# An H3 convolution with a bilinear GLU, forward and backward: product splits taken back and the last stage's order exchanged

## The chip, the cores and the metric

The kernel runs on one core of one Trainium2 chip. The metric is the device time of one execution in microseconds (us), smaller is better; a kernel is timed several times and the median is given. The profile is one further execution, taken by the hardware profiler.

## The reference

With x of shape 2048 x 512 in bf16, the reference computes a layer, and then the gradients of all nine inputs for a given output gradient `grad_out`. Cut to what matters:

```python
def _A_ref(q, k, v, shift_k, ssm_k, ssm_D):        # S = 2048, D = 512
    k_shift = sum(k_pad[:, t:t+S, :] * shift_k[:, 3-t] for t in range(4))
    kv = k_shift * v
    y = irfft(rfft(kv, 2*S) * rfft(ssm_k, 2*S))[:S] + kv * ssm_D   # a causal convolution over time
    return q * y

def _B_ref(x, w_gate, w_up, w_down):               # F = 1376
    h = (x @ w_gate) * (x @ w_up)
    return h @ w_down

xn = layernorm(x)
out = x + _A_ref(xn, k, v, shift_k, ssm_k, ssm_D) + _B_ref(xn, w_gate, w_up, w_down)
out, vjp = jax.vjp(_f, ...); grads = vjp(grad_out)
```

There are ten outputs: the layer's output, and the gradients for x, k, v, shift_k, ssm_k, ssm_D and the three weights.

## The kernel before

**Layout.** The 2048 rows are held as 16 row groups of 128 (R = 16); two neighbouring groups are a pair, n = 0 to 7. One SBUF array, `big`, holds everything, and tiles are places in it. PSUM is one array, `PP`, of eight banks of 512 f32 columns.

**Stages.** They overlap.
- `mlp_rows(j, r)`: F is cut into six steps j (widths 256, 96, 256, 256, 256, 256). For a pair of row groups a step computes the gradient through `w_down` (`pd`) and the gate and up products (`pg`, 512 columns for both), copies them out of PSUM and multiplies them into a ring of tiles; `hd_store` sends most of them to the DRAM array HD.
- `dw_gen(j)`: the weight gradients of step j, sums of products over the 16 row groups.
- `a_gen`, `s_B`, `s_pw`, `s_Bi`: the convolution, forward and backward, as a discrete Fourier transform in three steps with smaller tiles of the array (64x128, 64x32, 32x64); the results go through the DRAM arrays AX and CX.
- The last stage, in pairs n: `c_load(n)` brings pair n's part of CX into the one buffer `C` (1.5 MB); `last_dft(n)` makes three results of it with 24 products of shape 128x32; `c_dkv`, `c_y`, `c_o5` take them out and go on with them on ScalarE and VectorE; `c_dsk(n)` sums over the rows with 8 products of shape 128x32; `dk_pair` makes the gradient of k on VectorE. `hd_load(n)` reads pair n's part of HD with a transposing DMA into one of two buffers (`hdP[n % 2]`), `turn_gen` turns what was kept in SBUF, and `y_o(n, rr)` (11 products of 512 columns) and `y_x(n, rr)` (22) make the output and the gradient of x for the two row groups rr of the pair. `y_load`, `dkv_load` and `k_load` bring the other operands of 256 KB.

**Order.** All instructions are first recorded as 2271 entries; a run of products into one PSUM place with the same due time is one entry. `emit(PLAN)` then unpacks the constant `PLAN`: the order in which the entries are issued, and the PSUM bank of each of the 398 PSUM places. Each engine works through its entries in that order; waits between engines follow from the data and from places used again. All DMAs are issued by SyncE (SP) in the plan's order:

```python
raw = zlib.decompress(base64.b85decode(plan))
order = struct.unpack(f"<{len(ops)}H", raw[:2 * len(ops)])
for s, b in zip(slots, raw[2 * len(ops):], strict=True):
    s.base = Q[b // 2] if s.n == 2 else halves[b]
```

**Splits and fillers.** In step 3, and in step 4 for r < 8, `mlp_rows` makes the `pg` product in two halves of 256 columns. Ahead of the first data, the fillers multiply a tile of ones by itself: four products of 512 columns and eight of 256, then smaller ones.

Of the kernel before, what the change touches and what calls it, by code (L numbers as in the profile page):

```python
# [38 lines left out]
def kernel(  # L39
# [38 lines left out]
    Q = [PP[:, 1024 * i:1024 * i + 1024] for i in range(4)]  # L78
# [127 lines left out]
    MM = nc.tensor.matmul  # L206
# [44 lines left out]
    ones1 = rc.tile("ones", [128, 128])  # L251
# [11 lines left out]
    XT = rT.tile("XT", [128, 16, 1024])  # L263
    xnT = XT[:, 0::2, :].rearrange("p g (h c t) -> p g h c t", h=2, c=4)
# [21 lines left out]
    kh = ra.tile("kh", [128, R + 3, D])  # L286
# [28 lines left out]
    def wgu(j):  # L315
        return Wl[j % 2][:, 4 * SW[j]:12 * SW[j]].rearrange("p (c f) -> p c f", c=4)
# [6 lines left out]

    at0 = rN("P")
    now[0] = -50.0
    for i in range(12):
        w = 4 if i < 4 else 2
        MM(at0[:, 0:128 * w], lhsT=ones1[:], rhs=ones1[:].unsqueeze(1).to_broadcast((128, w, 128)), start=True, stop=True)
    for i in range(8):
        now[0] = -40.0 + i  # L330
        MM(at0[:, 0:128], lhsT=ones1[:], rhs=ones1[:], start=True, stop=True)
# [85 lines left out]
    def mlp_rows(j, r):  # L417
        fw = SW[j]
        h = ring(j, r, 2)
        if j:  # L420
            g = gu[(8 * j + r // 2) % 2].rearrange("p r (t f) -> p r t f", t=3)
            d = g[:, :, 2:3, :fw]
        else:
            g = gu0[r // 2 % 3].rearrange("p r (t f) -> p r t f", t=2)
            d = h[:, :, 0:1, :fw]
        pd = v3(rN(), 2)
        for rr in range(2):
            for c in range(4):
                MM(pd[:, rr, :fw], lhsT=goT[:, r // 2, c, 128 * rr:128 * rr + 128], rhs=wdT(j)[:, c, :], start=(c == 0), stop=(c == 3))
        (VCOPY if j in (3, 4, 5) else ACOPY)(d[:, :, 0], pd[:, :, :fw])  # L430
        for rr in range(2):
            pg = rN()[:, 0:2 * fw]
            for p in (slice(0, fw), slice(fw, 2 * fw)) if j == 3 or j == 4 and r < 8 else (slice(0, 2 * fw),):
                for c in range(4):
                    MM(pg[:, p], lhsT=xnT[:, r // 2, rr, c, :], rhs=wgu(j)[:, c, p], start=(c == 0), stop=(c == 3))
            ACOPY(g[:, rr, 0:2, :fw], pg.rearrange("p (t f) -> p t f", t=2))
        TT(h[:, :, 1:3, :fw], d.to_broadcast((128, 2, 2, fw)), g[:, :, 0:2, :fw], op=ALU.mult)
        TT(h[:, :, 0, :fw], g[:, :, 0, :fw], g[:, :, 1, :fw], op=ALU.mult)
# [143 lines left out]
    f = {}  # L582
# [251 lines left out]
    F0, F1 = 240.0, 415.0  # L834
    O0, OJ = 230.0, 10.0
# [60 lines left out]
    A = Gen(a_all())  # L896
# [42 lines left out]
    for n in range(NCH):  # L939
        last = n + 1 == NCH  # L940
        t = F0 + n * DF
# [30 lines left out]
        else:  # L972
# [4 lines left out]
            if n + 2 < NCH:  # L977
                y_load(n + 2)
                hd_load(n + 2)
    emit(PLAN)  # L980

# [106 lines left out]
```

## Time and profile before

| what | us |
|---|---|
| median of 3 runs (lowest, highest) | 426.84 (425.93, 427.25) |
| the profiled execution's own time | 426.57 |
| its span, first to last instruction | 424.4 |
| TensorE products (PE), busy | 415.1 |
| VectorE (DVE), busy | 349.0 |
| ScalarE (ACT), busy | 261.5 |

The page has the busy time of each engine (part 1), the span in 40 slices of 10.6 us with the busy share in tenths (part 2), the chain of work that ended last (part 4), and the costliest groups of instructions (part 5). In a group's row, "x1228 | 288.9, 380" means 1228 instructions, 288.9 us busy together, 380 ns from start to end of one; products overlap, so the mean is longer than their spacing. In a row of waits, "2.1, 2, 1.7" is the sum in us, how many, and the longest. In a timeline row come the start, the duration, the engine and the instruction; "L173" is the helper line through which every instruction is issued, so the tiles tell what it is. "SPq" is SP's queue: the time in which it issues a DMA. "PEld" is the weight load of a product.

### The profile page before, as it was taken

To read this page: it belongs to the slowest core of one execution; us is meant where nothing else is said; L and a number is where in the kernel's file an instruction comes from. 1 tells how busy PE (TensorE), PEld (TensorE's weight loads), DVE (VectorE), ACT (ScalarE), POOL (GpSimd) and SP (SyncE) were. 2 spreads that over 40 slices of the span, in tenths; PEclk is the share of its full clock that TensorE was granted. 3 is DMA by queue.
4 is the path that set the end of the run, shared out by engine and by line. 5 is a ranking of instruction groups with operands and counts; after the bars stand their busy time and mean duration, and the time that the engine had idled before them with its cause. 6 is when DMAs were issued, how large, how long until landed. Compare 5 with 4: busy or idle time off the path is not lost.

```text
span 424.4 us, 8338 instructions
## 1 busy us (share of the span) xinstructions
PE 415.1 (98%) x3290; PEld 209.3 (49%) x3290; DVE 349.0 (82%) x653; ACT 261.5 (62%) x380; POOL 3.5 (1%) x9
## 2 busy tenths in 40 slices
PE   8999999999999999999999999999999899999995
PEld 5755555855675444544444344445444344444443
DVE  5999977998649989899999990325858799999996
ACT  4855988598644999888999953362525331323324
POOL 1000000000000000000000000000000000000000
PEclk9999999999999999999999999999999999999999
DMA  7989999999788869968878899999999999999964
GB/s 262 398 197 379 320 306 388 349 367 365 288 310 287 319 229 352 313 227 318 319 274 344 292 312 325 298 348 274 231 275 329 303 269 329 308 302 286 267 193 144
DMA packets 104366, 127.27 MB, mean 300 GB/s; under 512 B 63876, under 2 KB 74249, under 8 KB 103304
## 3 DMA queue, kind: packets, MB, share of 16 engines
q1 hardware_dynamic: 104328, 126.75, 93.5%
q8 instruction: 25, 0.41, 0.4%
q14 instruction: 13, 0.11, 0.1%
HBM read 57.10 MB, written 54.04 MB: 262 GB/s over the span
## 4 chain that ended last, share of the span: by engine, by line
PE 77%; DMA 10%; DVE 10%; issue 1%; SPq 1%; ACTq 0%; ACT 0%
PE PP L173 77%; DVE big L173 10%; DMA out_dram<-big 4%; DMA big<-CX 2%; DMA big<-in_k_dram 2%; SPq L173 1%; DMA big<-in_w_dram 1%; DMA big<-in_go_dram 1%; ACTq L1084 0%; ACT big L173 0%
## 5 line engine op out<-in xcount | busy, mean ns | idle before, releaser
L173 PE MATMUL PP<-big 128*128 128x512 bf16 (+8 forms) x3290 | 415.1, 345 | 4.3 <-DMA big<-CX 2.1
L173 PEld LDWEIGHTS <-big 128*128 128x128 bf16 (+4 forms) x3290 | 209.3, 97 | 209.7 <-issue 61.0
L173 DVE TENSOR_TENSOR big<-big 128x1024 bf16<-128x1024 bf16 (+2 forms) x465 | 267.7, 631 | 45.5 <-ACT big L173 36.6
L173 ACT CAST big<-PP 128x512 bf16<-128x512 f32 (+2 forms) x314 | 224.4, 780 | 82.1 <-PE PP L173 71.1
L173 ACT ACTIVATE big<-big 128x1 f32<-128x1 f32 (+3 forms) x46 | 23.6, 522 | 53.4 <-DVE big L173 50.5
L173 DVE CAST big<-PP 128x512 bf16<-128x512 f32 (+1 forms) x37 | 32.4, 875 | 9.8 <-PE PP L173 5.2
L173 ACT COPY big<-PP 128x1024 bf16<-128x1024 bf16 x15 | 14.9, 1010 | 18.3 <-PE PP L173 18.3
L173 DVE SCALAR_TENSOR_TENSOR big<-big 128x512 bf16<-128x512 f32 (+2 forms) x36 | 23.3, 654 | 0.2
L173 DVE SCALAR_TENSOR_TENSOR big<-big,PP 128x512 f32<-128x512 bf16 x14 | 9.6, 684 | 9.2 <-PE PP L173 9.2
L173 DVE BATCH_NORM_STATS2 big<-big 128x6 f32<-128x512 bf16 x16 | 10.6, 682 | 4.0 <-DMA big<-in_x_dram 3.9
L173 DVE TENSOR_TENSOR big<-big,PP 128x512 bf16<-128x512 bf16 x14 | 9.2, 683 | 1.5 <-PE PP L173 1.5
L173 POOL MEMSET big<- 128x1536 bf16 (+2 forms) x3 | 2.9, 950 | 252.4 <-PE PP L173 252.4
L173 DVE TENSOR_SCALAR big<-big 128x512 bf16<-128x512 bf16 (+1 forms) x13 | 4.6, 385 | 0.0
L173 ACT ACTIVATE big<-PP 128x512 f32<-128x512 f32 x2 | 1.2, 597 | 4.5 <-PE PP L173 4.5
L173 DVE BATCH_NORM_AGGREGATE big<-big 128x2 f32<-128x6 f32 x16 | 2.3, 169 | 0.1
L173 ACT ACT_TABLE_LOAD x1 | 1.3, 1283 | 0.7 <-PEq L1076 0.7
L173 DVE RECIPROCAL big<-big 128x2 f32<-128x2 f32 (+1 forms) x9 | 1.2, 151 | 0.6 <-ACT big L173 0.6
L173 DVE DVE_READ_ACCUMULATOR big<-big 128x1 f32 x16 | 1.3, 82 | 0.0
L173 DVE DVE_READ_ACCUMULATOR big<-big,PP 128x1 f32 x14 | 1.2, 82 | 0.0
L173 DVE MEMSET big<- 128x128 bf16 (+1 forms) x2 | 0.2, 112 | 0.8 <-PEq L1076 0.8
L173 DVE COPY big<-PP 128x1024 bf16<-128x1024 bf16 x1 | 0.7, 692 | 0.2 <-PE PP L173 0.2
L173 ACT ACTIVATION_READ_ACCUMULATOR big<-PP 128x1 f32 x2 | 0.4, 194 | 0.0
(6 smaller groups left out, 0.9 us busy)
## 6 DMA issues: line engine op xcount, KB each, us to landing
HD<-big SPq DMA_DIRECT2D x32, 384.0 KB, 5.4
AX<-big SPq DMA_DIRECT2D x16, 768.0 KB, 5.6
big<-AX SPq DMA_DIRECT2D x16, 768.0 KB, 6.0
CX<-big SPq DMA_DIRECT2D x16, 768.0 KB, 5.4
out_dram<-big SPq DMA_DIRECT2D x43, 256.0 KB, 3.8
big<-CX SPq DMA_DIRECT2D x7, 1536.0 KB, 8.0
big<-in_vK_dram SPq DMA_DIRECT2D x8, 512.0 KB, 5.1
big<-in_w_dram SPq DMA_DIRECT2D x4, 768.0 KB, 7.5
```

Source lines behind the costliest of these rows:

```text
L173: o.fns.append(lambda: f(*[fix(x) for x in a], **{kk: fix(x) for kk, x in k.items()}))
```

## The change

Three edits:
- The splits of the `pg` products are taken back: one product of 512 columns for each of the four parts c, in all steps.
- The first fillers are eight products of 512 columns.
- `PLAN` is another one. Unpacked, the first 1575 of its 2271 entries stand in the same order with the same PSUM banks; behind them, every engine's and SP's order is another one, and 55 of the later PSUM places have another bank. It was chosen by its mean over drawn courses of the execution. No work is added or left out apart from the splits.

```diff
-PLAN = "c-l=@V-RM$vTb+9wr$(CZQHhO+qP}nHjZbGjlseD...
+PLAN = "c-l=@V-zMyuZ~k=+qP}nwr$(CZQHhOn~Rw>XV#ee...
...
-    for i in range(12):
-        w = 4 if i < 4 else 2
-        MM(at0[:, 0:128 * w], lhsT=ones1[:], rhs=ones1[:].unsqueeze(1).to_broadcast((128, w, 128)), start=True, stop=True)
+    for i in range(8):
+        MM(at0[:, 0:512], lhsT=ones1[:], rhs=ones1[:].unsqueeze(1).to_broadcast((128, 4, 128)), start=True, stop=True)
...
             pg = rN()[:, 0:2 * fw]
-            for p in (slice(0, fw), slice(fw, 2 * fw)) if j == 3 or j == 4 and r < 8 else (slice(0, 2 * fw),):
-                for c in range(4):
-                    MM(pg[:, p], lhsT=xnT[:, r // 2, rr, c, :], rhs=wgu(j)[:, c, p], start=(c == 0), stop=(c == 3))
+            for c in range(4):
+                MM(pg, lhsT=xnT[:, r // 2, rr, c, :], rhs=wgu(j)[:, c, :], start=(c == 0), stop=(c == 3))
```

The places of the new order that the prediction speaks of, from the unpacked entries (others left out):

```
PE before: ... last_dft(3) c_dsk(1) y(2) ... c_dsk(2) last_dft(4) y(3) ... c_dsk(7) y_o(7,0) y_o(7,1)
PE after:  ... last_dft(3) c_dsk(2) y(2, all 66 products) last_dft(4) c_dsk(3) y(3) ... y_o(7,0) y_o(7,1) c_dsk(7)

SP before: ... hd_load(3) ... c_load(4) y_load(3) dkv_load(4, v) ... hd_load(4) ...
SP after:  ... y_load(3) c_load(4) ... hd_load(3) ... hd_load(4) dkv_load(4, v) ...
```

More of the change, by code (lines that the diff above doesn't have):

```diff
@@ new lines @@
+PLAN = "c-l=@V-zMyuZ~k=+qP}nwr$(CZQHhOn~Rw>XV#ee&VGOHshm2gbo8W8cTxbEAPF#(fE17tia`Pp$O0uHJ|u>OfRG%DgMxuWfG7|ZqCqK$4l$rKB!iex7GgmnC<E=GBb0;K5C?KWTqq9}AQfzcc#s?BLmt=!9iS6*hSZQB3P1~J1q&c4<b^a)5V}BX$O?s^Fyw==&<(mn5vUDap&1l~me3sPLJz0|J)s^{gP|}3>O&Q%4h^6xq=QB<3}!-Os03|bB8-R1Fc=!b5U2s;pb7MXiZBg^!w9GehhaLLfmN^zn!+g910!JqtcFQ28g@fl=m%+GFZ6~LkQ2thEXaacaUbl5*{~9hz&%Keec&u4!Glm8lVS~=3v*x|B*O!62(n>KTm$`KE%b$2m>qwB$*>OA!(tc!f64c-1O~zeSO|+?D{O{aunp3~IrtHl!cUL^wm?R>0KY<XTn5|WXE+a2;3DjR<B$zbz<sy`Iq)dFgKO{zj=^I{jwc}no`RJ49&+MkNQJi{HU0wELGU|x4QVhf-hc;i6Vl;bNRPQN17^gBkO}X=bI1&t@g?NOPv8~Q#yqH)7Y$!PcK8<@0Rz^-x`>z$+d)07kH15HjDiKQAU43?pdo&MLU<KEg~AvW8)0Mo1D-+=Y=Y~sDXzy2xDo$^7PtxjhL+e0TVosi9Gc-@&=z;XHjIIzaST3zH_#5F;bv@)9k4lm1|2abZo$KN1jl16?1Y`M3wFf`*bU?0QDm$IU&32BhJVXf&>hF(7cd!PV-6UH|G;+ai9PTe_!_3-G@OXXaSryv>DU{$VjrA~eQ^rTz<xLh7vK(Dh%@m7?!=SWA7|kJ9EiJd5I&_LG#FRlE*ye!aUL$ip|}#4;4mDHOK~U-f-_hY=i>-`2Fr06Er(V#664`2T#T!+H7&x^*pL!pF>FM|u`wmU_}GT(({NggO{gukpk}lO8_+52OiigJoy9Ix0%y{BEQuGe6qd%0R0hvsCmKQRs4QN>L|6{5;B_Rtfj6-{UdF3f0dL`LtcbJm4vwTzbQde(LaL1SunJbii`bm*V>Nt$4{<NXqyzW}ALA2zim|9YjlyR*i(*q8ic8ONHod@?c!}cCD}0S}=n(G5Pw-Rx4C7M*`WzEdBAQEYa31xeRFs?Y&|un!sVNP;#l-XlmZAQXmabu0nonQiS6Ghn(x1|S#?WQTN98F$RiIu}fWF3W@LRkBNhlqqr;3z;Dp6AU4!_5-l#w#g75V`S(vO&#l2IYbLRqOY{e(Z`JIqG!@fZ9Rvr}QpLBC;gDneE0cf3k}U{T6Re`0SMP1ook{)K<zKbV64#Sd7Fic?i8K|n}EOw~weDy%^zBd6+=k^<GB1yqxwP)W)~QK=L~qpnnoYEx;7PW9+IEv9aCgX&NZ>O)ItDQ%=>)R(%`INC(xX$Nhi0W^W0(L~x#18FTyqUW@e*3%1GN0aF#ZJ=GWg{IInnnAbdFm0x(bdXNN5!z3$XgcktL-alEp#yZ3R?rW0jP}ycbdy%nJGw}#X%#J}AL%DLMc=|1dQGS4Q+hz}=`5|G6ZDuKk?=3{2|c8f^dtgOIUT2G=FcbtXXLk(i8J#X`kb=x7nGHMqpftC?$J5=ow9LuK2LWj2j8Wf{1@fozbQ96e@S0c9v;eH(S7=c@-pzZ6qk|XaSYDK#(&T-{*#9DZ2p%<@Jx=z|H?l!lK+v4Jc?s-d>+lwISP;A0z923aRQFYGk5~W;@Dh?EAuR#!xOm*CuGxtT!<(0IIhY;_mL~;cuvHLIr55h3Mb*hT#dh@4^o7SGV4@c!qs^Z72~8_mtv5p>LQM!$#^Lz=jfV(qv--ZPQ|$dm*l7#Qy21Lj-hchCD-71+L_~ODNd!SI5n5%_?kv*axE^yu{5@()-+s}%kdye%Lz20mglrun=5c)O{a-8spjW8+=Y{9U9QLJHM!R344P3Ja5C-6-MBla&>q~7dvXrVq>Z>S=hR-DQsZzzZNj~|DL3QhoJ$GDa&B$Gt2nPN=dIk5GwU+Wqg8btZ{up(iVNvnZq0qT4Y%dh+?T6sR?V*cxTvn=Y`TuK=o-$i>v=8r=fYZB^XULCqIL8wf59cR9hcJfTuh5=N!`wM^-JEtWweIY(w<aPOKUkTuLHRQ-{%KhLCfkxe#C>gfIjAm+L51dC2g#Oxt><hr`(B~>N9@MFZe5NqA$6!w$TRqHE-Zo+(=(@Tm6I^>Zkk}x6@|&4S&upw7quHZ}~f}uix_z+(DB_QkljBw7GWFWYR@{<W`zoQb;!)q$#DdZsb%lP`hd`9j4uNxQ@_WoLbVzKJKk)<pA&JA)HQn>Q6jaf98XnUi#_~ZK-?s9cPfCx|c`lW<Jb4bPM;<aXLYB$sx`m{WPQW*YP@Cb4n&@trIo3yywg^S!d`@&L-I<i{z1CxS0IPlXSKgm(_ZX*J@t5K<D`aU*t=?MlbVdy~3sBDv!}1b99#eO7nCR&(yIxSC4bx(y~CK$Rdp@>+}Sl<oUW@N9hKQCQG!0T;mnGQK#rsjV`CSq%70xe1l`iLS3a>bg`b{n6gQ4a#@Kb%XPCJ)?2(%KhQS4%`14R9@XFYDDTiae2nk%cKw~FX>8e}W#o|F<GuO^pXPlUNAgJxIij`X2%psaQd3TAZP}@D<t*>gLULSpYXONTC-j(}(mPsL&T2u4FMo1jNg($$p%j%wvYY4gUtCQR%UwOAH?_L#*T4Cep4Wr=4<FESa$B$IzkEX<=ylzyMdY%c)ADjvKkx;uB$u>;RF*6HP(dn6D|w`K<f4A6kF}Ygw3a9OnLgF~+FYJ#Re7T=q=7V&D$-J(>sR`TwvmR?SYGOD{X!qf3vDZ}^c($L@5y%>`Nhev`dEI~dh%A^@H_cU@5=-EQbm5yhw`<m{GspVFRd@#q^bO=->OMFap@pW<$G-+f9pH_S)WKp$twTozxrN((eCm=dq^jFBR}dd@{@KJu(#4)$a>0W65Y^xiP`58&3cPl7wIE?C8j--U~I2M?YYFYuF_BXOAHfxA@MDaMYY!w#nReK86ffOSNTHHS$g|T2Ff5AEMLkHiDg42l?{{FmcSC)8A)SFZKj-+bCSr;OKQtti7mNZkc*PUGTJP;B*|>H%#lo%(ms*Qc3G~-6Pqh3?5fO@{FcSCS~e?a^Ci12kZZC~uFE3HX^Z8x<+H+;!*baVazj3qqL$kVSRUIgd2NY&Bg5sX6}OW1os5vjc2jOi5gRE>Wtsdax8--)BW10a6|&{BLQ32BQo>fr9VuhaZIqO<a#r3(%W7FE-%3>*BYUNqRkTlRpX`_FHdfZiTB%?MWSy*+8a7TISvz}S<7I+Olu0sKYFSO&AnmP#b+jomRVvv*IV4r=YuPB9WV39Mx>nEX+cY_5b*!@0wg%SF8d+o8D%)hcG_j^Oz&hDsIU+~pm<+T*cHE}R&$2^0TNmqU-K@Lyu%0&2CfQ{BN@mDTd1kw0iXE2|a#BvoX?baX$Y5(`&8>yCv{u&3dRrgsYyGUXwXwD~)u!2Wn_)xj3;WcD+Dw~evu&9DYr}1h&9%?$bNkNj$_N{2qinSGx6St6ezLdry?tZ9*cRJrKiW_7#!lHQJ7Z&PkuA0*w$zr{X&Y<fY@U5-^KF4Gv|p{b|6o7cJKJX4ZHMi&Z*94)u$A_;{cdM%m+iJaw%7LAemh{RY_+YigLcRc+gclM6KtKWw+*(@HrXE*{7*~lzgaZ@%QAW<zhOu0oZYm4ETt#)WS+v$n|O53>@obP#q?Mn+vB);T#x6;{eqcC@r#zl|F*22&D|4tR4?EKJ-es!Bu<{j(|S6;WI4UEckuGw(K~r-@9gZUy|I_@lAgoU`yIP%MZCGU@Cts{K3G%#%Hn%MFXg$skmvRcUeT-jEi3Bzy_uKxGM>-NdKE9{x2=Y^@wVR16L}u5>9xFzclAnM+v|8Y@8NkJysp>t{@%a`_+W48>wLYp^7h`{dwNyx<-@(27xR_A$_x8IU+u$ujgRp9-o!`xDDUmle7eu@(LTl-`Zyo&6MT`+^jW^aC;1hd?8|(%_w^-?e$|%x6rbZ0{hD33jlRh@`xc+;{d}m8^{u|$8~IV+>&tzgAMtIz!*}{IpXYo0GauqF{d0fg$NhxQ_gDVfulNFA=%08WKj>Het$*QP`cxm}Cw;9i_EWyXzw)nrmw)TK{Tu(zulaSq;Wzz)-}2jj*B|-m$i@4N@AtEQ&VTare$g*^^6=CzJBCC4y+8BE{)Zp-6d`4xz#&z*<M%v-C?RTy79RM0|J|SX5B|dc^ync*_}M@8m?3p|=Mw(%=iVfw328&RkUnGx8AHhsEBx(oLa9(X{OS)qQ8?f~`ak}!CkelK#ZW0!4j)`Y!r&o($P_XM3-7&PC=_CcxS>oa91@2jA#11-s)lMIS;!TdhGwC9s1dS+Y$0jL9h!%hp;jmw;)U!XPbeFH@m3*cXdT*wwxL}Z8}f%@p?D}4?%92-8ES_UmLoI>?L+y{Aq)+}LV{2tbPRRF@Gvek44p#fFg{EO6T_s?FH{I!Lf$YU^bP&P<gh+83Ijs@P#{bRbwZD@A#4nrLeDTTObeUCmhiw@gg#+VSQX}m)nRHF83u>xVMgd4x`o+cYd9E2g>7L-7#-Gx1z}-0X^X<1@X)r0wPA7S8pebrVMkaR8i#q|TDTr=gqz`3xE+>-b)jC!7v_YW;Z8Ud4u>P*XgC&ThI`?7xEpqb^PyK*9`1*8VQ<(M_J@;Ucjz4+gjwN0xDZZ+i{Vtb6ds1t;aPYd9)-){On4Elgva4Ycp6@Yv*Bu(A6A5w0nJb&(>icuIA(Da5c5dO5{@v&>dxlEZX_ScganAtAz}%@9+^>{Bgg;b5sGZ)5r1e*ZV~VQNr>R1IYcf}h6qj^F-D_^Aksi1Rwj|@T$B|};bQ}j93#;|A@WI~M#5=Cjma<~LKlc=Tcm3vL{c(Pix@|kh!hOPBgP-eO)=vBe=9=tU&N0|8vO_8Bb@(0StP}X(trDZ3Iq{I@c-9G+5etKa{eD)`{>4$ID%hMfg@TG@bWQ~MDR!QjFd_uHHst}VLsN1KGrI7cZn35BIrD#sX`Hyk*fS3k1B-%"
```

1 line of the change is left out of this document (removed).

## The prediction

> **What bounds the kernel now.** I read the page first (busy time, slices), then what PE waited for, then SP's own waits, the chain of the last stage, and rows of single shapes. "F step j" in the change means step j of `mlp_rows`; n counts the eight row pairs of the last stage.
>
> The page, parts 1 and 2:
>
> ```profile
> PE 415.1 (98%) x3290; PEld 209.3 (49%) x3290; DVE 349.0 (82%) x653; ACT 261.5 (62%) x380; POOL 3.5 (1%) x9
> ...
> PE   8999999999999999999999999999999899999995
> ...
> DVE  5999977998649989899999990325858799999996
> ...
> PEclk9999999999999999999999999999999999999999
> DMA  7989999999788869968878899999999999999964
> ```
>
> PE is the bound: it works in 98% of the span at full clock. It runs from 8.09 us to 419.38 us almost without a gap, so the time is the sum of its products, the few waits inside, and 5.0 us of tail. In the last ten slices DVE and DMA are nearly full as well, so there a wait can come from either. What PE waited for, all of it:
>
> ```profile
> PE PP L173 <- DMA big<-CX: 2.1, 2, 1.7
> PE PP L173 <- DVE big L173: 1.1, 1, 1.1
> PE PP L173 <- DMA big<-in_w_dram: 0.9, 1, 0.9
> PE PP L173 <- DMA big<-in_go_dram: 0.2, 1, 0.2
> ```
>
> The last three lie before 34 us, in the part whose order stays. The first is the last stage: 1.73 us at 338.03 and 0.39 us at 395.73, both in front of `last_dft`. The timeline of SP around the first:
>
> ```profile
> 320.03 8.65 SPq L173 DMA_TRANSPOSE big<-HD  x1
> ...
> 329.41 0.53 SPq L173 DMA_DIRECT2D big<-CX  x1
> ```
>
> `hd_load(3)` held SP's queue for 8.65 us, and `c_load(4)`, whose buffer was free from the end of `last_dft(3)` (322.0 us), was issued only at 329.41. It landed at 337.99. SP's own waits show the other limit of this queue:
>
> ```profile
> SPq L173 <- DMA big<-CX: 12.4, 4, 4.2
> ```
>
> SP waits for loads that it issued itself: the trace has eight semaphores in turn, so a transfer is issued only when the eighth before it has landed. The shapes:
>
> ```profile
> L173 PE MATMUL PP<-big 128*128 128x512 bf16 x1228 | 288.9, 380 | 1.3 <-DVE big L173 1.1 <-DMA big<-in_go_dram 0.2
> ...
> L173 PE MATMUL PP<-big 128*128 128x256 bf16 x550 | 69.6, 276 | 0.9 <-DMA big<-in_w_dram 0.9
> ```
>
> The windows (PE and PEld come first after the length) of a stretch that has only 256 columns, of one that has only 512, and of the last stage:
>
> ```profile
> 113.67:119.77 6.10, 6.10 (x57) 5.47 (x56) 2.93 (x5) 1.17 (x2) 0.00 (x0) 1.00 0.61 198
> 303.00:320.40 17.40, 17.40 (x83) 7.87 (x81) 11.18 (x23) 4.62 (x7) 0.00 (x0) 1.00 1.01 275
> ...
> 320.00:419.00 99.00, 96.88 (x607) 43.84 (x606) 93.84 (x173) 34.06 (x52) 0.00 (x0) 1.00 1.03 280
> ```
>
> And the timeline at `c_dsk(2)`, where the shape changes: the weight load, elsewhere under the running product, is idle for 0.42 us.
>
> ```profile
> 335.68 0.12 PEld L173 LDWEIGHTS <-big 128*32 128x32 bf16 x8 [0.42 <-issue]
> ```
>
> **The change part by part.** The sum is made against the profiled execution, 426.57 us (span 424.4, 2.2 around it); the median of the three runs is 0.27 higher, 426.84.
>
> *Product splits.* Step 3 (16 groups) and the first half of step 4 (8 groups) lose four products each: 96 fewer, twice 256 columns becoming once 512. In the two windows of one shape the starts are 109.2 ns apart at 256 columns and 215.8 ns at 512 (6.10 us by 56, and 17.48 us, from start to start, by 81). A pair costs 218.4, a whole 215.8: 2.6 ns x 96 = 0.25 us. The rows' shares (126.5 and 235.3 ns) would give 17.7 ns and 1.7 us, but they count the end of a pipelined product on top. I take 0.25 us. PE is never idle there, so it arrives whole. The evacuation waits for both halves either way.
>
> *Fillers.* Twelve products of 4096 columns become eight of 4096 columns. At the cold start they are spaced by columns (427 ns at 512, 213 at 256), so they take as long: 0. PE then waits anyway (1.1 us for DVE, 0.9 for the first weights).
>
> *Order, shapes.* Unpacked as `emit` does it, the two orders are the same up to entry 1574 (251 us). Behind that, `c_dsk` stands beside a `last_dft` in seven of eight cases (before: in three), and both are 128x32. PE enters this shape 9 times instead of 13 and leaves it 8 times instead of 13 (the last `c_dsk` ends the program). In the starts, the last full product ahead of such a group takes 309.5 ns instead of 216 (+94), and leaving costs 105 + 10 ns. So 4 x 94 + 5 x 115 = 0.95 us less.
>
> *Order, the waits that go.* `c_load(4)` now stands ahead of `hd_load(3)`, and 66 full products lie between `last_dft(3)` and `last_dft(4)` instead of 54 (+2.6 us). The 1.73 us go. `c_load(7)` has 59 products before its reader instead of 55 (+0.9): the 0.39 goes too. Together 2.1 us; 0 if the queue is late again.
>
> *Order, the waits that come.* Each lies with a transfer that the new order puts further back, so I price each from both sides.
> (a) `hd_load(3)`, now behind `c_load(4)`, for the first product on pair 3. Before: issued 320.03 as pair 1's last product ended, landed 331.52, first read 334.73: 3.2 us to spare in 14.7. After: from pair 1's end to pair 3's first product PE has two `last_dft` (1.4 each), two `c_dsk` (0.55 each), 66 products (14.3) and two turns (0.45 each), 19.1 us, so 4.4 more. Against it, `hd_load(3)` cannot be issued before `last_dft(3)` has ended (1.4), and it queues behind `c_load(4)` (in the trace 5.2 to 6.2 us from the landing before a `c_load` to its own) and up to four loads or stores of 256 KB that used to be behind it (landings 0.65 apart: 0 to 2.6). To spare: 3.2 + 4.4 - 1.4 - (5.2 to 8.8), or 1.0 down to -2.6. I take 1.4 us of wait, past the middle (0.8), since a wait of this queue has gone to its late side here before (the 1.73 us).
> The Trainium skill, DMA: Bandwidth & Descriptors, Specifications, gives 435 GB/s for the fabric; by that figure the 1.57 MB of a `c_load` would hold the queue 3.6 us, (a) would end at 1.0 us of wait at most, and the sum would be some 1.2 us lower, 424.0. The 5.2 to 6.2 us measured here speak against it, and I do not use it.
> (b) `c_load(1)`: landed 281.43, read 282.43, so 1.0 us to spare. Two products fewer lie ahead of the reader (0.43), and the load's time of 9.1 us stood 1.1 above the row's median of 8.0. Wait 0 to 1.4; I take 0.6.
> (c) `hd_load(2)`, read right after `c_dsk(2)`: from pair 0's last product PE has 66 products (14.3), three turns (1.3), one `last_dft` (1.4) and one `c_dsk` (0.55), 17.6 us. The load can be issued some 2 us in (a store that waits for DVE's add stands before it) and needs 10.2 as before, plus what `c_load(3)`, issued about 3 us earlier, still holds of the queue (2.2 to 3.2) and two to four small transfers (1.3 to 2.6): 15.7 to 18.0. Wait 0 to 0.4, to 1.0 if `c_load(3)` is late too; I take 0.4.
> Together 2.4 us, bounds 0 and 5.0.
>
> *Tail.* Before, 5.06 us follow PE's end: a copy 0.37, an activation 0.81, a DVE add 0.42, queueing, and stores that land 2.0 us after issue. After, PE ends on `c_dsk(7)`; a copy of 128x512 (0.59) and a 4 KB store follow, behind three stores at 0.4 us each. The DVE adds of `dk_pair` and y_x(7) are fed 4.9 us before PE's end and need some 6 us there. I take 0.7 us less; bounds 0 and 1.2.
>
> Sum: -0.25 - 0.95 - 2.1 + 2.4 - 0.7 = -1.6 us. 426.57 - 1.6 = 424.97; on the median's scale 425.2.
>
> **Rivals.**
> *A, the new order runs clean.* No wait of (a) to (c): -4.0, 422.8 us. For it: every margin above reaches zero. Against: DMA is at 1.03 of its engines from 320 to 419 us. Chance 0.15.
> *B, the gain is eaten.* (a) at its worst, 2.6, (b) and (c) together 1.6: -4.0 + 4.2 = +0.2, 427.0 us. A product wait is only exchanged, CX for HD. Chance 0.22.
> *C, slower: DVE's data behind a transpose.* `dkv_load(4)` of v stood ahead of `hd_load(4)` (issued 330.53, landed 339.35); now it stands behind. `hd_load(4)` goes out when pair 2's last product ends (call it 0) and holds SP 7.6 us (5.1 of it its own, by the landings); then v needs 2.7 (idle queue) to 8.5 us (median row): 10.3 to 16.1. DVE then makes the `c_dkv(4)` product, three more at 0.6, and y_x(3,1)'s add (0.69): done 3.1 later, 13.4 to 19.2. PE needs that bank for y_o(3,0) after `last_dft(4)`, `c_dsk(3)` and 59 products, at 14.9. So it waits 0 to 4.3 us, from the point where v lands later than 11.8. At the far end: -1.6 + 4.3 = +2.7, 429.5 us. For it: DVE is busy 93.84 of 99 us there and cannot catch up. Against: the queue ahead is short. Chance 0.21. The Trainium skill, TensorE: Matmul & The Clock Gate, part 1, says that PE falls to half clock after an idle window of about 3.4 us; no wait here is that long (clock 1.00 through the 1.73 us). By that rule C at its far end would cost up to 1.7 us more, 431.2, by an estimate from the page.
>
> **How the numbers follow.** The forecast (new waits between 1 and 3.3 us, C's wait at zero) has 0.42, the rivals 0.15, 0.22 and 0.21. The forecast's own range is 424.2 to 426.5. Runs of this kernel differ by 1.3 us; 0.3% (1.28 us) is what a measurement can tell, so faster is below 425.56 and slower above 428.12. Faster: A and three quarters of the forecast, 0.15 + 0.32 = 0.47. Same: the rest of the forecast, 0.10, most of B, 0.14: 0.24. Slower: C and the rest of B, 0.29. The range for 8 in 10 goes from A's upper half to C's far end: 423.0 to 429.6.
>
> **What would show it.** Matmuls 3190 instead of 3290; starts of 216 ns in steps 3 and 4; PE at 250 us earlier by 0.25. No PE wait for CX at `last_dft(4)`; a wait for HD of 0 to 2.6 us ahead of pair 3. After PE's last product, about 4.4 us instead of 5.06. Wrong would be: a DVE wait on in_vK before `c_dkv(4)` with PE waiting for DVE at y_o(3,0) (C), waits for HD above 3 us (B), or none of either (A).

## The result, and the profile after

The change makes the kernel slower: 430.12 us (median of six, 429.00 to 431.87) against 427.19 us before; the ratio is 1.007 with a 95% interval of 1.0045 to 1.0095. Forecast was 425.2, range 423.0 to 429.6. A second set of runs, shown below, gave 1.0056 (1.0022 to 1.0089).

The profiled execution took 431.87 us (span 430.1), the longest of its six, so its waits are on the large side; a second profile is given where it matters. The page, parts 1 and 2:

```profile
PE 409.8 (95%) x3134; PEld 199.8 (46%) x3190; DVE 350.1 (81%) x653; ACT 261.7 (61%) x380; POOL 3.4 (1%) x9
...
PE   7999999999999999999999999989998898999796
...
DVE  4999968998659998999999950626677769999996
```

PE has less work and a longer span: 3190 products instead of 3290, as the weight loads count them. The records of 56 products are missing here, so 409.8 us is too low; the second profile has all 3190, with 413.8 us busy against 415.1 before. The loss is in the last 14 slices: PE's row there has sevens and eights where it had nines. What PE waited for, all of the span and then the last part of it:

```profile
PE PP L173 <- DVE big L173: 4.4, 4, 1.7
PE PP L173 <- DMA big<-CX: 3.9, 2, 2.2
PE PP L173 <- issue: 1.6, 10, 0.2
PE PP L173 <- DMA big<-in_w_dram: 1.4, 1, 1.4
PE PP L173 <- DMA big<-HD: 1.2, 1, 1.2
PE PP L173 <- ACT big L173: 1.1, 3, 0.8
```

Behind 250 us these are 9.0 us (CX 3.9, DVE 3.1, HD 1.2, ACT 0.8), where the kernel before had 2.1. PE's timeline gives their places (start, duration, and in brackets the idle time before and what ended it):

```profile
284.32 43.77 PE L173 MATMUL PP<-big 128*32 128x512 bf16 x302 [1.73 <-DMA big<-CX]
329.50 10.45 PE L173 MATMUL PP<-big 128*128 128x512 bf16 x82 [1.41 <-DVE big L173]
341.11 12.91 PE L173 MATMUL PP<-big 128*128 128x512 bf16 x57 [1.16 <-DMA big<-HD]
355.69 2.53 PE L173 MATMUL PP<-big 128*128 128x512 bf16 x11 [1.68 <-DVE big L173]
359.02 40.86 PE L173 MATMUL PP<-big 128*128 128x512 bf16 x240 [0.79 <-ACT big L173]
402.05 2.23 PE L173 MATMUL PP<-big 128*32 128x512 bf16 x27 [2.17 <-DMA big<-CX]
```

In order these are `last_dft(1)`, `y_o(2,0)`, the first product on pair 3, `y_o(3,0)`, `y_o(4,1)` and `last_dft(7)`. The releasers differ, but one queue issues all the transfers behind them. SP's timeline in the middle of the stage:

```profile
302.97 0.53 SPq L173 DMA_DIRECT2D big<-CX  x1
...
305.79 12.49 SPq L173 DMA_TRANSPOSE big<-HD  x1
318.38 0.53 SPq L173 DMA_DIRECT2D big<-in_x_dram  x1
...
321.17 0.45 SPq L173 DMA_DIRECT2D out_dram<-big  x1
...
322.13 0.99 SPq L173 DMA_DIRECT2D out_dram<-big  x2
326.19 0.34 SPq L173 DMA_DIRECT2D big<-in_x_dram  x1
326.62 0.38 SPq L173 DMA_DIRECT2D big<-CX  x1
...
327.96 11.07 SPq L173 DMA_TRANSPOSE big<-HD  x1
...
340.23 8.01 SPq L173 DMA_TRANSPOSE big<-HD  x1
348.28 0.57 SPq L173 DMA_DIRECT2D big<-in_vK_dram  x1
```

`hd_load(2)` holds SP for 12.49 us. Before, with no `c_load` just ahead of it, it held 6.61:

```profile
302.06 6.61 SPq L173 DMA_TRANSPOSE big<-HD  x1
```

`hd_load(3)` rises from 8.65 to 11.07; the eight together from 69.0 to 81.0 us. All that stands behind a held queue is late, not only the transfer that is held. An entry that waits for data delays those behind it too: `c_load(4)`, whose buffer was free when `last_dft(3)` had ended (about 320.4), went out at 326.62, because `y_load(3)` ahead of it waited for the store of `y_o(1)`, issued at 321.17 behind `hd_load(2)` and landed at 326.18. DVE's timeline shows two more of the victims:

```profile
327.56 1.29 DVE L173 TENSOR_TENSOR big<-big 128x1024 bf16<-128x1024 bf16 x2 [1.91 <-DMA out_dram<-big]
...
352.41 2.62 DVE L173 TENSOR_TENSOR big<-big 128x1024 bf16<-128x1024 bf16 x4 [2.35 <-DMA big<-in_vK_dram]
```

The second is v of pair 4, issued at 348.28 behind `hd_load(4)`, landed at 352.32. The first is a store: `c_dkv(3)` writes `dv`, a single buffer, and must wait until the store of pair 2's `dv` has landed. That store was issued at 322.13, behind `hd_load(2)` and seven others, and landed at 327.46; in the kernel before it went out at 310.02, the second of these two:

```profile
309.39 2.18 SPq L173 DMA_DIRECT2D out_dram<-big  x2
```

PE then waits for DVE at `y_o(2,0)` and `y_o(3,0)`.

**The account** of the two profiled spans, 430.1 - 424.4 = +5.7: waits in the last stage 9.0 - 2.1 = +6.9; PE ahead by 0.22 at the same product near 248 us; fewer shape changes (forecast 0.95, about 0.9 by the halved pair below); from the start of PE's last product to the end of the span 4.44 instead of 5.33, -0.89. That is +6.9 - 0.22 - 0.9 - 0.89 = +4.9, so 0.8 is missing. Some 0.6 of it lies in the counting, by an estimate: a row's idle time begins at the modelled end of the product before it, 0.38 us after that product's start, while without a wait the next one would start 0.216 us after it. So each of the four additional waits costs about 0.16 us more than its row says. The rest was not found.

### The profile page after: what moved, and what is told of

Same layout as the page of the kernel before. It is cut to its first block, busy times and chain, and to the rows that moved or that the text cites. A ratio compares the mean times of both kernels' runs of the same rounds, so it can differ in the third digit from the quotient of the medians.

```text
span 430.1 us, 8079 instructions
## 1 busy us (share of the span) xinstructions
PE 409.8 (95%) x3134; PEld 199.8 (46%) x3190; DVE 350.1 (81%) x653; ACT 261.7 (61%) x380; POOL 3.4 (1%) x9
## 4 chain that ended last, share of the span: by engine, by line
PE 70%; DMA 12%; DVE 9%; SPq 4%; issue 3%; ACT 1%; DVEq 0%; ACTq 0%
PE PP L173 70%; DVE big L173 9%; DMA big<-CX 5%; SPq L173 4%; DMA big<-HD 3%; ACT big L173 1%; DMA big<-in_w_dram 1%; DMA out_dram<-big 1%; DMA big<-in_vK_dram 1%; DVEq L173 0%; ACTq L173 0%
## 5 line engine op out<-in xcount | busy, mean ns | idle before, releaser
L173 PE MATMUL PP<-big 128*128 128x512 bf16 (+8 forms) x3134 | 409.8, 350 | 16.2 <-DVE big L173 4.4
L173 PEld LDWEIGHTS <-big 128*128 128x128 bf16 (+3 forms) x3190 | 199.8, 97 | 225.7 <-issue 61.5
L173 DVE BATCH_NORM_STATS2 big<-big 128x6 f32<-128x512 bf16 x16 | 10.6, 682 | 4.2 <-DMA big<-in_x_dram 4.1
```

What stands on the lines that cost most here:

```text
L173: o.fns.append(lambda: f(*[fix(x) for x in a], **{kk: fix(x) for kk, x in k.items()}))
```

## The experiments

**Theory (queue):** SP's queue is the cause. A transposing load keeps SP until what was issued ahead of it has landed and some more; the new order puts these loads behind `c_load`s, SP is held longer, and loads and stores behind it come late for PE and DVE. **Rival (engines' order):** the new order of PE, DVE and ACT itself makes them late. **Second rival (full DMA engines):** the hold of SP is no more than a sign that the 16 DMA engines are full; it is taken up at the halved pair.

**The splits alone**, `e1_splits` and, again, `r_splits`. The `PLAN` of before with the changed products and fillers:

```diff
 PLAN = (that of before)
-            for p in (slice(0, fw), slice(fw, 2 * fw)) if j == 3 or j == 4 and r < 8 else (slice(0, 2 * fw),):
+            for c in range(4):  # one product of 512 columns, fillers 8 x 512
```

> The kernel before with its own order, and only the product splits and the fillers changed. Queue theory (the loss is all in the last stage, from SP's queue: the eight hd_load held SP 81.0 us after, 69.0 before): -0.2 to -0.3 us against the kernel before, 3190 products, PE waits in the last stage as before (about 2.1 us for CX), median near 426.9. Rival, splits matter (a whole product of 512 columns is evacuated later than two halves, and DVE or ACT then keep PE waiting in steps 3 and 4): 1 us or more slower than before.

> The kernel before with only the splits and the fillers changed, again, beside the run of the tail. The sum of the prediction: 0.25 us faster than before; the first run had 1.2 us (interval 0.3 to 2.1), with the CX wait at last_dft(4) at 0.3 instead of 1.7 us. If that wait's size is chance, the second run lies between 0 and 1 us faster and the wait anywhere from 0 to 2 us; if the splits' 0.25 us moves the queue into a better course, again 1 us or more faster and the wait under 0.8 us.

Measured: 425.18 us against 426.69 (ratio 0.9972, 0.9951 to 0.9993), and the second time 427.75 against 427.24 (1.0005, 0.9979 to 1.003). Between the same two products, near 58 and 248 us, PE takes 190.34 to 190.35 us in the three profiles with splits, and 190.12 to 190.14 in six of the 13 without (up to 190.50 in the others): 0.23 us, as costed. What the first run gained beyond that did not come again, and is put down to chance: PE's wait at `last_dft(4)` was 0.3 us in the first profile, 2.0 in the second. No loss comes from the splits. In the changed kernel the stretch that held 57 products before (x57) has 30, mostly of 512 columns, with PE as full (window: length, then PE):

```profile
113.45:119.55 6.10, 6.10 (x30) 2.78 (x29) 2.96 (x5) 1.17 (x2) 0.00 (x0) 1.00 0.70 246
```

**SP's order alone**, `e2_sp_order`: before's order on PE, DVE and ACT, the changed order on SP.

> The kernel before (splits and fillers kept, order of PE, DVE and ACT kept, PSUM places kept) with only SP's transfers of the last stage in the changed kernel's order. Queue theory: slower than before by 2 to 5 us, hd_load(2) and hd_load(3) hold SP for 11 to 13 us instead of 6.6 and 8.7, and PE waits for HD, for DVE or for CX in pairs 2 to 4 by 3 us or more together. Rival, engines' order (the new order of PE, DVE and ACT makes the loss, SP's merely follows): within 1 us of before.

Measured: 459.64 us (1.0772, 1.0742 to 1.0802). Far beyond either expectation, and it does not tell them apart: in the new sequence a transfer waits for results that the old engine order makes late (`c_load(3)` was issued at 313.88, in the changed kernel at 302.97), and PE waited up to 10.01 us at once. Behind three such waits the profile has 23.9 us at half clock, up to 12 of the 33 us that were lost. SP's sequence fits only the engine order it was made for.

**Single transfers moved in the changed kernel.** `e3_v4` and `e4_hd2`:

```
SP, e3_v4:  ... hd_load(3) dkv_load(4).ks dk_pair.st  dkv_load(4).v  hd_load(4) ...
SP, e4_hd2: ... hd_load(2)  c_load(3) ... y_o(0).st dkv_load(3).v y_load(2) ...
```

> The changed kernel with one transfer moved on SP: dkv_load(4) of v ahead of hd_load(4) instead of behind it. Queue theory: v lands 8 us or more before 352.3, DVE's wait of 2.35 us for in_vK goes, PE's 1.68 us for DVE at y_o(3,0) and the 0.79 for ACT behind it go; 1 to 2.5 us faster than the changed kernel (430.1), 427.6 to 429. Rival (DVE is late at that place by its own load of work): the PE wait at y_o(3,0) stays above 1 us, the time within 0.5 of 430.1.

> The changed kernel with one transfer moved on SP: hd_load(2) ahead of c_load(3) instead of four places behind it. Queue theory: hd_load(2) holds SP 7 to 9 us instead of 12.5, the stores and loads queued behind it are issued earlier, PE's 1.4 us for DVE at y_o(2,0) goes and the 1.2 us for HD before pair 3 shrinks; c_load(3) lands about 320, 0 to 1 us after last_dft(3) could start; 0.5 to 2 us faster than the changed kernel. Rival (a hold is a fixed time of the transposing load, whatever stands ahead): the hold stays at 11 us or more and the wait at y_o(2,0) stays.

`e3_v4`: 429.12 us (1.0063, 1.0039 to 1.0087), no gain that can be told from the 1.007 and 1.0056 of the changed kernel. DVE's wait for in_vK is gone, but another stands in its place, for the store of `dv` of pair 3 behind `hd_load(4)` (2.80 us for out_dram at 350.87), and PE still waits 0.81 us at `y_o(3,0)`. `e4_hd2`: 432.74 us (1.0143, 1.0101 to 1.0185), slower, against the expectation. Its hold did what the theory says:

```profile
306.85 7.76 SPq L173 DMA_TRANSPOSE big<-HD  x1
```

7.76 instead of 12.49: a hold is no fixed time. But `c_load(3)` now went out 11.7 us later (314.66 instead of 302.97) with all that stands behind it. The profiled execution took 438.76 us, 6 above the median, so only the hold and the times of issue are read from it.

**The changed kernel again, and three moves at once**, `r_after` and `e5_dv`:

```
SP, e5_dv:  ... hd_load(2)  c_dkv(2).st  y_load(2) ... hd_load(3)  c_dkv(3).st ... dkv_load(4).v  hd_load(4) ...
```

> The changed kernel again, unaltered, on the chip of the three runs beside it. All theories: 429.5 to 431 us; the same places of PE wait (last_dft(1), y_o(2,0), pair 3's first product, y_o(3,0), last_dft(7)), each different by up to 1 us from the first profile, since the landings move by as much.

> The changed kernel with three transfers moved on SP: the stores of dv of pairs 2 and 3 right behind hd_load(2) and hd_load(3) instead of seven and five places behind, and dkv_load(4) of v ahead of hd_load(4). Queue theory, now with its second half (dv is one buffer: c_dkv(n+1) on DVE waits until the store of c_dkv(n) has landed, and that store stands behind a transposing load): DVE's waits for out_dram of 1.9 us at 327.6 and of 2.8 us at 350.9 (in the run with v alone) go, PE's waits at y_o(2,0), y_o(3,0) and y_o(4,1), 4 us together in the profile of the changed kernel, fall under 1 us; 2 to 4 us faster than the changed kernel. Rival (DVE's own order is late there, the store is only the last of several): the waits at y_o(2,0) and y_o(3,0) stay above 1 us each, under 1 us faster.

`r_after`: 429.52 us against 427.55. The same places wait, by 2.9 us for CX, 1.6 for DVE, 1.1 for HD and 0.8 for ACT: 6.4 us. `e5_dv`: 428.61 us (1.0023, 0.9995 to 1.0052), 0.9 better than `r_after`, with intervals that overlap, and not the 2 to 4 expected. In its profile 3.41 us went by at half clock behind the wait at `last_dft(1)` (on this below). The two stores landed 4.7 and 10.6 us earlier, and DVE then stood before the next late transfer at the same instructions:

```profile
328.50 1.29 DVE L173 TENSOR_TENSOR big<-big 128x1024 bf16<-128x1024 bf16 x2 [1.15 <-DMA big<-KS]
...
353.25 2.02 DVE L173 TENSOR_TENSOR big<-big 128x1024 bf16<-128x1024 bf16 x3 [2.21 <-DMA out_dram<-big]
```

**c_load hurried**, on top of `e5_dv`: `e6_dv_c7` (right behind `hd_load(6)`), `e8_c7t` (behind the turning load), `e9_c1` (as `e8_c7t`, and `c_load(1)` ahead of two stores):

```
SP, e6_dv_c7: ... hd_load(6)  c_load(7)  c_dkv(5).st y_load(6) turn_gen(12) ...
SP, e8_c7t:   ... hd_load(6)  turn_gen(12)  c_load(7)  c_dkv(5).st y_load(6) ...
SP, e9_c1:    ... hd_load(0)  c_load(1)  dw.st dw.st ...
```

> As the run before, and c_load(7) right behind hd_load(6) instead of six places further back. Queue theory: c_load(7) is issued 3 to 4.5 us earlier, PE's 2.2 us for CX at last_dft(7) goes; another 1 to 2.2 us, 425 to 427.5 in all. Rival (the load lands when the DMA engines are free, not when it is issued): it lands within 1 us of where it did, and the wait stays above 1 us.

> The changed kernel with dkv_load(4) of v ahead of hd_load(4), the two stores of dv right behind their hd_load, and c_load(7) ahead, but behind the turning load (DMA big from big) that the run before pushed too late. Queue theory (every place given to one transfer is taken from the next): the 4.2 us wait for big goes, c_load(7) lands 2 to 5 us before 402, PE's CX wait at last_dft(7) under 0.7 us; the other waits as in the run with v and dv; 426.5 to 428.5. Rival (a load can be hurried only once; the next late one is as dear): a wait of 1.5 us or more for another transfer appears in pairs 6 and 7, time as the run with v and dv.

> As the run beside it, and c_load(1) ahead of the two stores of the weight gradients behind which it stood. Queue theory: c_load(1) is issued 1 to 2 us earlier and lands 2 us earlier (the two stores took 2.3 us of the queue), PE's 1.6 to 2.2 us at last_dft(1) falls under 0.5; ACT or DVE may wait for the stores instead, up to 1 us; 425 to 427.5, up to 2 us faster than the run beside it.

All three are slower than `e5_dv`: 432.55 (1.0113), 433.15 (1.0132) and 434.89 us (1.0164). Each time the hurried load came in time and another transfer took its place. `c_load(7)` landed at 392.70 in `e6_dv_c7`, 7.9 us earlier than in `e5_dv`, and PE waited for the turned tile; in `e8_c7t` DVE waited for `y_load(6)`, and PE for DVE; in `e9_c1` ACT waited for the stores that had been put back, and PE for ACT. Part of these times is the clock: the three profiles have 3.41, 6.83 and 3.41 us at half clock behind such waits, which is worth up to half of that. One line of each (what PE waited for; DVE's timeline; PE's timeline):

```profile
PE PP L173 <- DMA big<-big: 4.2, 1, 4.2
```

```profile
395.29 0.69 DVE L173 TENSOR_TENSOR big<-big 128x1024 bf16<-128x1024 bf16 x1 [6.21 <-DMA big<-in_x_dram]
```

```profile
285.85 14.37 PE L173 MATMUL PP<-big 128*32 128x512 bf16 x107 [3.26 <-ACT big L173]
```

The expected gains failed here, in the way that the expectation of `e8_c7t` has it, and more strongly than its numbers: a place given to one transfer is taken from the next. How much of the loss is this and how much the clock is not separated.

**One exchange alone**, `e7_swap`: `r_splits` with `c_load(4)` ahead of `hd_load(3)`.

> The kernel before with the splits and fillers changed and its own order, and one transfer moved on SP: c_load(4) ahead of hd_load(3), as the changed kernel has it. The prediction's rival B: PE's CX wait at last_dft(4) (1.7 in the profile of before, 0.3 in the run with the splits alone) goes, and a wait for HD of 1 to 2.5 us ahead of pair 3 takes its place; within 1 us of the run with the splits alone, hd_load(3) holds SP for 10 to 11 us instead of 8.6. If the exchange were free: no wait at either place, 0.5 to 1.5 us faster than the splits alone.

Measured: 428.10 us (1.0014, 0.9989 to 1.0039), no better than the splits alone (0.9972 and 1.0005). The wait for CX at `last_dft(4)` is gone; `hd_load(3)` is held for 11.95 instead of 8.6 us, and PE waits for HD. SP's timeline, then what PE waited for:

```profile
322.39 0.33 SPq L173 DMA_DIRECT2D big<-CX  x1
322.77 11.95 SPq L173 DMA_TRANSPOSE big<-HD  x1
```

```profile
PE PP L173 <- DMA big<-HD: 1.8, 1, 1.8
```

That is rival B's exchange, shown alone.

**The queue relieved**, `e11_after_half` and `e12_before_half`. The move experiments left it open whether SP's time is the common cause. So both kernels were run with half of what `hd_load` transfers:

```diff
-        ldT(out=hdP[n % 2][:, :, 0:b - a], in_=HP[n, a:b])
+        h = (b - a) // 2
+        ldT(out=hdP[n % 2][:, :, 0:h], in_=HP[n, a:a + h])
```

> The changed kernel with every hd_load reading only the first half of its rows of HD (the other half of each pair's tile keeps what lay there, so out and the gradient of x are left uncomputed in part); all else as it was. Queue theory: the eight holds fall from 81 us to under 50, PE's waits in the last stage fall from 7 to 9 us to under 3, and the time is 422 to 425 us: the prediction's terms that do not hang on the queue (splits 0.25, shapes 0.95, tail 0.7) are then what is left, so 0.5 to 2.5 us faster than the kernel before with the same halving. Rival (the order of PE, DVE and ACT makes the waits): waits of 4 us or more stay, and the changed kernel stays 1 us or more slower than the halved kernel before.

> The kernel before with the same halving of hd_load (the same part left uncomputed). Queue theory: holds fall from 69 us to 40 to 50, the CX wait at last_dft(4) goes, PE's waits in the last stage under 1 us; 423.5 to 426 us. Rival: as the kernel before, and the halved changed kernel above it.

Measured, side by side: the changed kernel 422.35 us (ratio to the whole kernel before 0.9885, 0.9863 to 0.9907), the kernel before 423.76 us (0.992, 0.9895 to 0.9945). The order of the two turns over: the changed one is now 1.41 us the faster. The holds are 50.8 and 38.3 us. What PE waited for behind 250 us, changed kernel and kernel before:

```profile
PE PP L173 <- DMA big<-CX: 0.6, 1, 0.6
PE PP L173 <- issue: 0.2, 1, 0.2
```

```profile
PE PP L173 <- issue: 1.1, 7, 0.2
```

With the order of PE, DVE and ACT untouched, 9.0 (or 6.4) us of waits fall to 0.6 (the rows of `issue` are places of missing records). So the engines' order does not make the waits by itself; they come with the load on the transfers.

What the pair does not show is which limit of the transfers it is. Halving relieves SP's queue, and with it the DMA engines. The windows of the last stage, of the changed kernel, then of the halved changed kernel and the halved kernel before (the last three numbers are the granted clock, the DMA share and GB/s):

```profile
320.00:419.00 99.00, 91.22 (x545) 41.13 (x548) 88.36 (x166) 31.17 (x45) 0.00 (x0) 1.00 1.01 271
```

```profile
320.00:419.00 99.00, 95.33 (x568) 44.36 (x575) 93.18 (x174) 34.18 (x53) 0.00 (x0) 1.00 0.83 232
```

```profile
320.00:419.00 99.00, 96.37 (x600) 44.06 (x608) 94.44 (x175) 35.01 (x54) 0.00 (x0) 1.00 0.78 232
```

The share falls from 1.01 (before: 1.03) to 0.83 and 0.78. And while SP is held the DMA engines are not idle. The windows of the holds of `hd_load(2)` and `hd_load(6)` in the changed kernel:

```profile
305.79:318.28 12.49, 12.44 (x71) 6.13 (x70) 9.01 (x15) 3.74 (x5) 0.00 (x0) 1.00 1.13 283
...
376.51:387.99 11.48, 11.43 (x76) 5.03 (x76) 11.38 (x24) 3.50 (x5) 0.00 (x0) 1.00 1.05 276
```

With a share of 1.13 and 1.05 there, it stays open whether the hold of SP or the full DMA engines are the limit. The single moves show that the place in the queue decides which transfer is late (`c_load(7)` in `e6_dv_c7`, issued 6.6 us earlier than in `e5_dv`, landed 7.9 us earlier). No run issued transfers from a second queue, which could tell the two apart.

This pair also measures what is left without the waits. From the same product near 248 us to the start of PE's last product it takes 168.1 - 0.6 of wait = 167.6 us after and 168.5 before: 0.9 us for the shape changes. From there to the end of the span it is 4.47 and 5.33: 0.86 us for the tail. With the 0.23 of the splits this is 2.0, less 0.57 of wait: 1.4, the difference of the medians.

**The tail alone**, `e10_tail`: `r_splits` with its last 60 entries in the changed kernel's relative order.

> The kernel before with the splits and fillers changed, and the last 60 entries in the changed kernel's relative order: c_dsk(7) last on PE, DVE's y_x(7) ahead of the last of dk_pair, the o4 store last. The prediction's tail term and one shape change: from the start of PE's last product to the span's end 4.7 us instead of 5.4, 0.5 to 1.0 us faster than the run of the splits alone. If the tail's gain needs the earlier order of DVE too: within 0.3 us of it.

Measured: 425.80 us against 427.24 (0.9952, 0.9927 to 0.9977): 2.0 us faster than the splits alone beside it (427.75), more than expected, though its interval overlaps that of their first run (0.9972). Why is not settled: in the last stage its profile has 2.7 us of waits of PE, against 3.9 with the splits alone, and such waits vary by chance. The time from the start of PE's last product to the end is 5.68 us in it, not the 4.7 expected (5.32 with the splits alone), since DVE still works until 423.99, 2.4 us past the start of PE's last product (0.8 in the changed kernel).

## Why the prediction was wrong, step by step

- *Splits, -0.25:* right, 0.23 between the same two products. The sign that was given for it, PE ahead at 250 us, proves little: PE was 0.22 ahead there in the first profile and 0.26 behind in the second, since the first products come at different times (the same product near 58 us at 56.9 to 59.7 us over the runs). *Fillers, 0:* nothing shows against it, within that scatter.
- *Shape changes, -0.95:* right, 0.9 in the halved pair.
- *Tail, -0.7:* inside its bounds, 0.89 and 0.86 from the start of PE's last product, 1.0 from PE's end (5.06 to 4.06); that it can be had by itself is not shown.
- *Waits that go, -2.1:* half wrong. CX at `last_dft(4)` went, though `c_load(4)` was itself late. The 0.39 at `last_dft(7)` grew to 2.17: I counted the products ahead of the reader (+0.9) and not that SP, held by `hd_load(6)` for 11.48 us with six entries queued behind it, would issue `c_load(7)` at 392.61 instead of 387.10. SP's timeline, before and after:

```profile
387.10 0.68 SPq L173 DMA_DIRECT2D big<-CX  x1
```

```profile
392.61 0.66 SPq L173 DMA_DIRECT2D big<-CX  x1
```

- *(a) `hd_load(3)`, 1.4:* right in size, 1.16 and 1.1, but by luck in part. Before, this load went out at 320.03 not because pair 1's last product had ended (about 317.1) but because the eighth transfer before it, `c_load(3)`, landed at 319.97. After, it went out only at 327.96, more than 8 us past pair 1's end (about 319.2), behind the late `c_load(4)`; the sum has no such term. The prediction's side sum with 3.6 us for a `c_load` does not come out either: it leaves 3.2 + 4.4 - 1.4 - (3.6 to 6.2), so no wait at all, and 423.8 instead of 424.0.
- *(b) `c_load(1)`, 0.6:* 1.73 and 1.5, above its bound of 1.4. It was issued 3.3 us later (275.57 instead of 272.31), behind `hd_load(0)`, held for 9.03 instead of 7.47 us, and stores; the sum has neither. *(c) `hd_load(2)`, 0.4:* 0, inside its bounds.
- *C's mechanism* (v behind `hd_load(4)`, given 0.21 as an alternative) came, with 1.68 us and 0.79 behind it; v landed 14.3 us after pair 2's last product (338.04), within the 10.3 to 16.1 worked out. But I listed it as a case that excludes the forecast, where its price simply adds to it.
- *Not seen:* the store of `dv` behind `hd_load(2)`, 1.41 us at `y_o(2,0)`.
- *The forecast's own range, 424.2 to 426.5,* does not follow from its new waits of 1 to 3.3 us: -4.0 + 1 and -4.0 + 3.3 give 423.8 to 426.1.

The term that failed is the sum of new waits: 2.4 us forecast, against 9.0 in the last stage of the profiled run (6.4 in the second). The reason is one step: I priced each transposing load by when it lands for its own reader, and took its hold of SP from the kernel before as it was. The holds grew from 69.0 to 81.0 us (78.6 in the second profile), with what stood ahead, and all that stood behind were late by it. Only six transfers were followed, out of some hundred in the stage, with DMA at 1.03 of its engines and one queue for all. The halved pair shows that the load on the transfers makes these waits; whether a held SP or full DMA engines set the limit stays open.

The prediction took half clock as out of reach, since no wait of 3.4 us was to be seen. In the changed kernel that held: behind PE's waits of 1.73 us and 2.17 us the granted clock stayed at 1.00. But it is not a safe reading. Behind a wait of 3.47 us in `e8_c7t` the clock was 0.50, and in `e5_dv` it was 0.50 for 3.41 us behind a wait of only 2.12 us at `last_dft(1)`. In `e9_c1` a wait of 3.26 us cost no clock. The Trainium skill, TensorE: Matmul & The Clock Gate, part 1, which the prediction cited for half clock after an idle window of about 3.4 us, does not foretell this if the window is taken for the length of one wait, and the measurement decides: a wait of 2.12 us was followed by half clock too. The windows of the changed kernel behind 2.17 and 1.73 us, of `e8_c7t` behind 3.47 and of `e5_dv` behind 2.12 us (the third number from the end is the clock):

```profile
402.10:405.00 2.90, 2.90 (x32) 1.21 (x33) 2.05 (x4) 2.28 (x4) 0.00 (x0) 1.00 0.97 197
```

```profile
284.90:288.20 3.30, 3.25 (x41) 1.52 (x31) 0.69 (x1) 2.50 (x3) 0.00 (x0) 1.00 1.02 368
```

```profile
403.20:406.00 2.80, 2.80 (x13) 0.79 (x13) 2.80 (x7) 1.12 (x3) 0.00 (x0) 0.50 0.86 203
```

```profile
284.90:288.20 3.30, 3.30 (x30) 1.06 (x23) 0.83 (x2) 2.22 (x3) 0.00 (x0) 0.50 0.98 341
```

## What to carry to other kernels

When one queue issues everything and is nearly full, price a new order by the time the queue is held, and follow every transfer behind a held one, stores included: a store that lands late stops the engine that wants its buffer. Waits found in this way add up; they are not alternatives. To see whether the transfers are the cause at all, make the dearest one smaller in both kernels rather than move transfers about; that does not yet tell a held queue from full DMA engines.

## What the runs showed of the hardware

In these profiles a transposing load holds the issuing queue by what is in flight ahead of it. In the profiles of the kernel before and after, the hold ended 3.8 to 5.4 us (n below 4, 1152 rows) or 2.7 to 2.9 us (n from 5 on, 896 rows) after the last landing ahead, with 2.9 and 3.9 for `hd_load(4)`: `hd_load(3)` 328.68 behind a landing at 324.58 before, 339.03 behind 334.98 after; `hd_load(7)` 399.82 behind 397.02 and 406.03 behind 403.34. Other runs have up to 7.5 us for `hd_load(2)`. So the same load cost SP 6.61, 7.76 or 12.49 us. In the last stage the waits move by 1 to 2 us from one execution to the next: with the same program, the splits alone, `last_dft(4)` waited 0.3 us in one profile and 2.0 in the other, which is as much as most single edits here were worth.
